# Retention and a low-rank mixer on one core: the second batch's unit work and the third batch's loads rearranged

## The chip, the core and the metric

The kernel runs on one core of one Trainium2 chip. A core has TensorE (PE in the profile: matrix products and transposes; PEld is its weight load), VectorE (DVE), ScalarE (ACT), GpSimd (POOL) and SyncE (SP), each with its own queue of instructions, and 16 DMA engines that all queues share. The metric is the device time of one execution in microseconds; the median of several runs is compared. One more execution was profiled, and all places and durations in this text come from its trace.

## The reference

```python
scores = q @ k^T / sqrt(64)                    # per batch (8), head (8); 576 positions, 64 wide
gamma  = 1 - 2 ** (-5 - head)
ret    = scores * (gamma ** (i - j) if i >= j else 0)
x      = ret @ v                               # heads side by side: (8, 576, 512)
h      = (x^T @ U @ V)^T                       # U: 576 x 32, V: 32 x 576
u      = x + h
out    = u + max(u @ w_ch1, 0) @ w_ch2         # w_ch1: 512 x 2048, w_ch2: 2048 x 512
```

The decay `gamma ** (i - j)` factors into a part for the query row and a part for the key row, so a key or a value can be scaled by its position before the product, and the result by the query's position after it.

## The kernel before, in words

Batches are taken in pairs. A pair has 2 x 576 = 9 x 128 rows, nine chunks; chunk 4 (called J) holds the end of the first batch and the start of the second. For pairs 1 to 3 each chunk is loaded (`load`, L227), cast (`cast_chunk`, L270), transposed by a DMA (`xbar`, L295) and used by `section` (L403: scores SC L312, values RV L332, running state). `prep` is cast and transpose together. The third batch is the first of pair 1; its chunks are `order[NI]`, `order[NI + 1]` and on.

Pair 0 is written out by hand in another form, so as to start early. The two batches are cut into four units of 256 rows, here called unit one to four (`u` = 0 to 3 in the code; units three and four are the second batch), and the chunk J. Unit work is:

- `load_u` (L621): k, q and v of a unit, each in two DMAs of 256 KB (four heads each), issued on SyncE. A memset by POOL into the first destination tile can hold them back: the DMA must wait for it, and what follows it on SyncE's queue waits too.
- `scale_u` (L653, instruction L655): the keys of four heads times a decay, f32 to bf16. `cast_u` (L646, L651): q or v of four heads to bf16.
- `T_u` (L662): transposes of k or q by TensorE (L671) into PSUM. With an engine named, all 16 land in one PSUM tile, which that engine copies out (L683 ScalarE, L685 VectorE). Without one they land in two tiles, copied by ScalarE (L680) and VectorE (L681) side by side. The PSUM tiles come from `ps_big`, three of them, which the Y1 blocks use as well.
- `SC_u` and `mask_u` (L700, L708): scores and their mask; `ST_u`, `Sblk` (L779, L789): the running state; `RV_u`, `QS_u`, `XS_u` (L727, L762, L770): values, the state's share, and the result scaled.

The feed-forward part is done per batch: 16 Y1 blocks (`u @ w_ch1`, L531, then Relu by ScalarE, L536), one for 128 columns of w1, and then Y2 (L565). w1 and w2 are loaded by POOL's own DMA queue (`load_w1` L196, `load_w2` L200), which converts f32 to bf16; `load_w1(f0, f1)` brings the columns of blocks f0 to f1 - 1. A Y1 block waits for its piece of w1.

`startup` (L881) has the first batch's units and all loads. Its loop at L947 is POOL's work for units three and four, with w1's pieces between, and then w2. `first_stretch` (L1003) is the second batch: `y(n)` puts the next n Y1 blocks of the first batch between the steps of `unit` (L1025), which has unit three and then unit four. Before it, L1049 issues the third batch's first loads (k, q and v of three chunks, k and q of a fourth) on SyncE, right behind unit four's. `merge` (L1083) then goes through Y1 of the second batch and Y2 of both and puts the third batch's casts, transposes and sections at given shares of that work. Order on each engine is the order written (`manual_schedule`); the stage buffers for f32 inputs are 15, used in turn.

Of the kernel before, what the change touches and what calls it, by code (L numbers as in the profile page):

```python
# [34 lines left out]
def kernel(  # L35
# [11 lines left out]
    nc = tc.nc  # L47
# [10 lines left out]
    NI = 9  # L58
# [105 lines left out]
    def load_v_rows():  # L164
        nc.sync.dma_start(out=V_f, in_=moe_V)
# [28 lines left out]
    def load_w1(f0, f1):  # L194
        w = slice(f0 * P, f1 * P)
        nc.gpsimd.dma_start(  # L196
            out=w1_sb[:, :, w], in_=moe_w_ch1[:, w].rearrange("(c p) f -> p c f", p=P))
# [16 lines left out]

    ch = {}

    def load(pr, i, which, seg=None):
        c = ch.setdefault((pr, i), {})
        for j in which:
            if ("f", j) not in c:  # L220
                c["f", j] = stage.tile([P, H, D], FP32, tag="stage", name="stage_t")
            dram = (q, k, v)[j]
            for n_seg, (rows, b, t0) in enumerate(parts(pr, i)):
                if seg is not None and n_seg != seg:
                    continue
                n = rows.stop - rows.start
                nc.sync.dma_start(  # L227
                    out=c["f", j][rows, :, :],
                    in_=dram[b, :, t0:t0 + n, :].rearrange("h s d -> s h d"),
                )  # L230
# [361 lines left out]
    order = [(pr, i) for pr in range(B // 2) for i in range(NI)]  # L592
# [53 lines left out]
    def cast_u(u, j, hh, eng):  # L646
        o, f = unit_views(u, j, hh)
        if eng is nc.scalar:
            nc.scalar.activation(out=o, in_=f, func=AF.Copy)
        else:  # L650
            eng.tensor_copy(out=o, in_=f)  # L651

    def scale_u(u, hh, eng):  # L653
        o, f = unit_views(u, 1, hh)
        eng.tensor_tensor(  # L655
            out=o, in0=f,
            in1=vscaleU[:, u, :, 4 * hh:4 * hh + 4].rearrange("p j h -> p h j")[
                :, :, :, None].to_broadcast([P, 4, 2, D]),
            op=ALU.mult,
        )  # L660
# [220 lines left out]
    def startup():  # L881
        load_u(0, (1, 0))
        load_v_rows()
        load_u(1, (1, 0))
        load_u(0, (2,))
        load(0, J, (1, 0), seg=0)
        load_u(1, (2,))
        load(0, J, (2,), seg=0)
        load_u_rows()
        load(0, J, (1, 0, 2), seg=1)  # L890
        load_u(2, (1, 0, 2))
        nc.gpsimd.memset(st["x", 0][HI, J, :], 0.0)

        warm(10)
        cast_unit(0)
        T_u(0, 1, nc.vector)
        un[0]["off"] = y1_tile(0)[:, 0:4, :].rearrange(
            "p (a x) (y i) -> p a (x y) i", x=2, i=P)
        nc.vector.memset(un[0]["off"][HI], 0.0)
        warm(5)  # L900
        nc.scalar.activation(out=V_b, in_=V_f, func=AF.Copy)
        T_u(0, 0, nc.scalar)
        make_v()
        warm(5)
        SC_u(0, 0, ps_sc, "psc")
        mask_u(0, 0)
        cast_unit(1)
        cast_u(0, 2, 0, nc.gpsimd)
        cast_u(0, 2, 1, nc.gpsimd)
        cast_u(1, 2, 0, nc.gpsimd)  # L910
        load_w1(0, 2)
        cast_u(1, 2, 1, nc.gpsimd)
        T_u(1, 1, nc.scalar)
        SC_u(0, 1, ps_o, "po")
        mask_u(0, 1)
        SC_off(0, ps_sc, "psc")
        warm(3)
        T_u(1, 0)
        SC_off(1, ps_o, "po")
        warm(3)  # L920
        SC_u(1, 0, ps_sc, "psc")
        mask_u(1, 0)
        cast_qk(0, J, LO, nc.scalar, nc.vector, decay=True)
        SC_u(1, 1, ps_o, "po")
        mask_u(1, 1)

        acc1 = pss_tile()
        ST_u(0, ALL, acc1, True)
        Sblk(acc1, 1)
        RV_u(0, 0)  # L930
        RV_u(0, 1)
        RV_off()
        XS_u(0)
        T_J(LO)
        acc2 = ps_big.tile([P, NHP, P], FP32, tag="big", name="pss2")
        ST_u(0, ALL, acc2, True)
        prep_v(0, J, LO)
        cast_urows()
        RV_u(1, 0)
        SC_J(LO)  # L940
        mask_J(LO)
        ST_u(1, LO, acc1, False)
        Sblk(acc1, 2)
        cast_qk(0, J, HI, nc.gpsimd, nc.gpsimd)
        prep_v(0, J, HI)
        load_w1(2, 4)
        for u in (2, 3):  # L947
            for hh in range(2):
                scale_u(u, hh, nc.gpsimd)
            load_w1(4 if u == 2 else 10, 6 if u == 2 else 12)  # L950
            for hh in range(2):
                cast_u(u, 0, hh, nc.gpsimd)
            load_w1(6 if u == 2 else 12, 8 if u == 2 else 16)
            if u == 2:
                load_u(3, (1, 0, 2), nc.gpsimd)
            cast_u(u, 2, 0, nc.gpsimd)
            cast_u(u, 2, 1, nc.gpsimd)
            if u == 2:
                load_w1(8, 10)
        for f in range(0, NF, 2):  # L960
            load_w2(f)
        RV_u(1, 1)
        QS_u(1, 0, 1)
        XS_u(1, 0, 1)
        ST_u(1, ALL, acc2, False)
        Sblk(acc2, 3)
        QS_u(1, 1, 2)
        XS_u(1, 1, 2)
        RV_J(LO)
        QS_J(3)  # L970
        XS_J(LO)

        xT = [ps_big.tile([P, dm], FP32, tag="big", name="xT") for _ in range(3)]
        xT.append(ps_sc.tile([P, dm], FP32, tag="psc", name="xT"))

        def to_xT(lo, hi):
            for i in range(lo, hi):
                for cc in range(NCC):
                    nc.tensor.matmul(
                        xT[cc][:, i * P:(i + 1) * P],  # L980
                        st["x", 0][:, i, cc * P:(cc + 1) * P], ident,
                        start=(i == 0), stop=True, skip_group_check=True,
                    )

        to_xT(0, 2)
        MA, _, _, _ = mixer_items(0, 0, split=True)
        MA((ps_o, "po"))
        to_xT(2, J)
        for cc in range(NCC):
            g = slice(cc * R, (cc + 1) * R)  # L990
            nc.tensor.matmul(
                xT[cc], st["a", 0][g, :], V4[g, HALF:HALF + 4 * P],
                start=False, stop=True, skip_group_check=True,
            )
        for cc in range(NCC):
            o = st["uT", 0][:, :, cc, :]
            i_ = xT[cc].rearrange("p (s t) -> p s t", t=P)
            if cc % 2 == 0:
                nc.scalar.activation(out=o, in_=i_, func=AF.Copy)
            else:  # L1000
                nc.vector.tensor_copy(out=o, in_=i_)

    def first_stretch():  # L1003

        ys = iter([fn for _, fn in y1_items(0)])

        def y(n):
            for _ in range(n):
                fn = next(ys, None)
                if fn is not None:  # L1010
                    fn()

        _, MH0, _, outs0 = mixer_items(0, 0, split=True)
        MA1, MH1, MT1, outs1 = mixer_items(0, 1, split=True)
        T_J(HI)
        y(1)
        make_u()
        SC_J(HI)
        mask_J(HI)
        y(1)  # L1020
        acc = pss_tile()
        ST_J(HI, acc)
        Sblk(acc, 0)

        def unit(u, slots, last):  # L1025
            T_u(u, 1, nc.vector)
            T_u(u, 0, nc.scalar)
            y(2)
            SC_u(u, 0, ps_sc, "psc")
            mask_u(u, 0)  # L1030
            y(1)
            ST_u(u, LO, acc, False)
            Sblk(acc, slots[1])
            SC_u(u, 1, ps_sc, "psc")
            mask_u(u, 1)
            y(1)
            if not last:
                ST_u(u, HI, acc, False)
                Sblk(acc, slots[2])
            RV_u(u, 0)  # L1040
            QS_u(u, 0, slots[0])
            QS_u(u, 1, slots[1])
            if last:
                RV_J(HI)
                XS_J(HI)
            RV_u(u, 1)
            XS_u(u)

        for g in range(NI, NI + 4):  # L1049
            load(*order[g], (1, 0, 2) if g < NI + 3 else (1, 0))  # L1050
        unit(2, (0, 1, 2), False)
        y(1)
        unit(3, (2, 3), True)
        y(1)
        MA1()
        y(1)
        MH1(outs1[0])
        y(2)
        MT1(outs1[0])
        MH1(outs1[1])  # L1060
        y(16)
        Y1, rest = y1_items(1, by_seg=True)
        Y1(0, 0)
        Y1(1, 0)
        MT1(outs1[1])
        MH0(outs0[0])
        Y1(2, 0)
        for f in range(3):
            Y1(f, 1)
        return rest[3:]  # L1070

    with tc.manual_schedule():
# [18 lines left out]
        g = NI + 7  # L1091
        for b in range(2, B):
            pr, par = divmod(b, 2)
# [37 lines left out]
```

## Time and profile before

| what | us |
|---|---|
| median of 5 runs (326.48 to 328.36) | 327.03 |
| the profiled execution's own time | 327.62 |
| its span, first to last instruction | 325.8 |
| TensorE busy | 312.0 (96%) |
| VectorE busy | 168.3 (52%) |
| ScalarE busy | 144.2 (44%) |
| POOL busy | 102.7 (32%) |
| Y1 products L531, 768 | 132.9 |
| Y2 products L565, 535 | 123.8 |
| L655 key scaling on POOL, 8, mean 1061 ns | 8.4 |
| L651 casts on POOL, 16, mean 645 ns | 10.1 |

Busy time is the sum of an engine's instructions; DMA issues do not count as busy. Times in the timelines are from the start of the span. The granted clock of TensorE was 1.000 over the whole span.

### The profile page before, as it was taken

How to read it: one execution, taken by the hardware profiler on the slowest of the kernel's cores; microseconds unless marked ns; L12 is line 12 of the kernel's file. 1: busy time of each engine (PE TensorE's matmuls, PEld its weight loads, DVE VectorE, ACT ScalarE, POOL GpSimd, SP SyncE). 2: the span in 40 equal slices, each digit the busy share in tenths (PEclk: the TensorE clock that was granted, in tenths of full speed). 3: DMA queues.
4: the chain of work that ended last, by engine and by line, in shares of the span. 5: the costliest groups of instructions: out<-in, count | busy, mean ns of one | idle time of the engine just before them, and what ended most of it. 6: DMA issues, size and time to landing. Idle time of an engine off the chain costs nothing.

```text
span 325.8 us, 9085 instructions
## 1 busy us (share of the span) xinstructions
PE 312.0 (96%) x3860; PEld 170.8 (52%) x3885; DVE 168.3 (52%) x332; ACT 144.2 (44%) x326; POOL 102.7 (32%) x171
## 2 busy tenths in 40 slices
PE   8998889999999999999999999999999999999996
PEld 3574545765444444456744444457644444467544
DVE  7664454427645477546754477555744476510012
ACT  3847547894011385038810484048800473047400
POOL 7587772243112733132321423142321500010000
PEclk9999999999999999999999999999999999999999
DMA  8999999999994988978997599969996440340012
GB/s 220 232 217 204 252 197 196 197 206 145 228 208 113 256 178 179 210 183 168 201 190 178 137 187 209 208 151 164 190 209 171 116 67 3 101 111 0 2 75 86
DMA packets 152904, 53.30 MB, mean 164 GB/s; under 512 B 132032, under 2 KB 150336, under 8 KB 152864
## 3 DMA queue, kind: packets, MB, share of 16 engines
q1 hardware_dynamic: 144512, 40.40, 66.6%
q0 software_dynamic: 8352, 12.32, 16.4%
q8 instruction: 30, 0.49, 0.7%
q14 instruction: 10, 0.08, 0.1%
HBM read 36.85 MB, written 9.44 MB: 142 GB/s over the span
## 4 chain that ended last, share of the span: by engine, by line
PE 76%; DMA 9%; SPq 5%; ACT 3%; DVE 2%; POOL 2%; issue 2%; DVEq 0%
PE ps_y L565 36%; PE ps_y L531 32%; DMA qkT<-qk 3%; SPq L633 3%; DMA w_sb<-in_moe_w_ch_dram 2%; DMA stage_t<-in_k_dram 2%; DMA stage_t<-in_v_dram 2%; PE pp L312 2%; DVE u L480 2%; SPq L227 1%; ACT y L536 1%; PE pp L332 1%; PE pp L344 1%; PE ps_y L576 1%; POOL qk L655 1%
## 5 line engine op out<-in xcount | busy, mean ns | idle before, releaser
L531 PE MATMUL ps_y<-uT,w_sb 128*128 128x256 bf16 (+2 forms) x768 | 132.9, 326 | 2.0 <-DMA w_sb<-in_moe_w_ch_dram 1.0
L536 ACT ACTIVATE y<-ps_y 128x384 bf16<-128x384 f32 (+2 forms) x192 | 89.6, 491 | 96.0 <-PE ps_y L531 94.9
L565 PE MATMUL ps_y<-w_sb,y 128*128 128x512 bf16 x535 | 123.8, 379 | 2.2 <-issue 1.1
L531 PEld LDWEIGHTS <-w_sb 128*128 128x128 bf16 x768 | 72.1, 98 | 50.0 <-issue 2.7
L565 PEld LDWEIGHTS <-y 128*128 128x128 bf16 x560 | 52.6, 98 | 61.1
L288 POOL TENSOR_TENSOR vt<-stage_t,vscale 64x256 bf16<-64x256 f32 (+1 forms) x81 | 50.2, 619 | 68.6 <-DMA stage_t<-in_v_dram 58.5
L554 DVE TENSOR_TENSOR o_sb<-ps_y,u 128x512 f32<-128x512 f32 (+2 forms) x38 | 25.2, 664 | 82.1 <-PE ps_y L565 79.8
L557 POOL DMA_DIRECT2D out_dram<-o_sb x31 | 17.2, 554 | 105.0 <-DVE o_sb L554 99.1
L320 DVE TENSOR_TENSOR ret<-pp,triH 128x512 bf16<-128x512 f32 x27 | 18.7, 692 | 24.0 <-PE pp L344 18.6
L480 DVE TENSOR_TENSOR u<-ph,xt 128x768 bf16<-128x768 f32 (+2 forms) x24 | 21.8, 951 | 5.9 <-PE ph L474 5.9
L279 DVE CAST qk<-stage_t 64x256 bf16<-64x256 f32 x54 | 19.1, 353 | 5.2 <-DMA stage_t<-in_k_dram 4.0
L453 ACT ACTIVATE a_sb<-pa 128x128 bf16<-128x128 f32 x8 | 2.2, 278 | 43.2 <-PE pa L447 43.2
L360 DVE TENSOR_TENSOR xt<-pp,qscale 128x512 bf16<-128x512 f32 x27 | 18.6, 690 | 4.7 <-PE pp L344 4.2
L399 DVE TENSOR_TENSOR s_sb<-AB,Af 64x256 bf16<-64x256 f32 x42 | 17.7, 422 | 2.1 <-ACT s_sb L394 1.5
L354 DVE COPY q<-qkT 64x256 bf16<-64x256 bf16 x48 | 13.2, 275 | 9.8 <-DMA qkT<-qk 8.8
L280 ACT ACTIVATE qk<-stage_t 128x512 bf16<-128x512 f32 x27 | 16.8, 621 | 0.6 <-DMA stage_t<-in_q_dram 0.6
L708 DVE TENSOR_TENSOR ret<-psc,triU 128x1024 bf16<-128x1024 f32 x8 | 9.7, 1222 | 9.7 <-PE psc L700 9.7
L392 ACT ACTIVATE Af<-AB 128x256 f32<-128x256 f32 x24 | 9.2, 385 | 8.1 <-PE AB L374 7.7
L651 POOL CAST qk<-stage_t 128x512 bf16<-128x512 f32 x16 | 10.1, 645 | 3.9 <-DMA stage_t<-in_v_dram 3.1
L312 PEld LDWEIGHTS <-qkT 64*64 64x64 bf16 x432 | 5.6, 107 | 10.8 <-issue 7.8
L277 ACT ACTIVATE qk<-stage_t 128x256 bf16<-128x256 f32 x27 | 11.0, 409 | 0.0
L655 POOL TENSOR_TENSOR qk<-stage_t,vscaleU 128x512 bf16<-128x512 f32 x8 | 8.4, 1061 | 5.4 <-PE psc L700 2.9
(121 smaller groups left out, 213.8 us busy)
## 6 DMA issues: line engine op xcount, KB each, us to landing
stage_t<-in_k_dram SPq DMA_DIRECT2D x32, 256.0 KB, 4.7
stage_t<-in_q_dram SPq DMA_DIRECT2D x32, 256.0 KB, 5.4
stage_t<-in_v_dram SPq DMA_DIRECT2D x32, 256.0 KB, 5.7
out_dram<-o_sb POOLq DMA_DIRECT2D x31, 256.0 KB, 3.5
w_sb<-in_moe_w_ch_dram POOLq DMA_DIRECT2D x14, 256.0 KB, 9.2
stage_t<-in_k_dram SPq DMA_DIRECT2D x8, 128.0 KB, 3.3
stage_t<-in_q_dram SPq DMA_DIRECT2D x8, 128.0 KB, 3.8
stage_t<-in_v_dram SPq DMA_DIRECT2D x8, 128.0 KB, 3.5
```

Source lines behind the costliest of these rows:

```text
L279: nc.vector.tensor_copy(out=o[to, hl], in_=f[fr, hl])
L280: nc.scalar.activation(out=c["qk"][:, 0, :], in_=c["f", 0].rearrange("p h d -> p (h d)"), func=AF.Copy)
L288: nc.gpsimd.tensor_tensor(out=o[to, hl], in0=f[fr, hl], in1=w[fr, hl, :, None].to_broadcast([n, NHP, D]), op=ALU.mult)
L320: nc.vector.tensor_tensor(out=ret.rearrange("p a b i -> p a (b i)").rearrange("p a (b i) -> p a b i", i=D), in0=pp[:, :, 0:NHP * D].rearra ...
L360: nc.vector.tensor_tensor(out=st["x", pr][:, i, :].rearrange("p (hp hl d) -> p hl hp d", hl=2, d=D), in0=pp[:, :, NHP * D:2 * NHP * D].rea ...
L399: nc.vector.tensor_tensor(out=S_[half(x), 1, :], in0=Bk[half(1 - x)], in1=Af[half(1 - x), now, :], op=ALU.add)
L480: nc.vector.tensor_tensor(out=st["u", par][:, i0 - base:i0 - base + n, w].rearrange("p s (c d) -> p c s d", c=2), in0=ph[k][:, :, 0:n, :], ...
L531: nc.tensor.matmul(ps[:, 0:n, :], w1_sb[:, cc, f * P:(f + 1) * P], st["uT", par][:, c0:c0 + n, cc, :], start=(cc == 0), stop=(cc == NCC - 1),)
L536: nc.scalar.activation(out=st["y1", par][:, f, c0 * P:(c0 + n) * P], in_=ps[:, 0:n, :].rearrange("p s t -> p (s t)"), func=AF.Relu)
L554: nc.vector.tensor_tensor(out=o_sb[:, 0:n], in0=ps[:, 0:n], in1=st["u", par][:, c, w], op=ALU.add)
L557: (nc.sync if last else nc.gpsimd).dma_start(out=out_flat[r0:r0 + P, w], in_=o_sb[:, 0:n])
L565: nc.tensor.matmul(ps, st["y1", par][:, f, c * P:(c + 1) * P], w2_sb[:, f, :], start=(f == 0), stop=(f == NF - 1),)
```

## The change

Five edits, all in the second batch's stretch:

- The keys' scaling of units three and four is split: heads 0 to 3 stay on POOL, heads 4 to 7 go to VectorE, unit three's after the first Y1 block of the stretch, unit four's after unit three's second mask.
- POOL's loop is written out in another order: w1 4-5 ahead of unit three's keys, unit four's loads behind w1 6-7.
- w1's blocks 8 to 11 come in one piece; before they came in two, the second behind unit four's keys.
- The first load of the third batch moves from L1050 into `startup`, behind w1 12-15, and gets a gate: a one-column memset by POOL, as unit four's loads have.
- q's transposes of units three and four use two PSUM tiles, copied by ScalarE and VectorE. One Y1 block fewer stands inside unit three, one more behind it; in unit four one of its two early blocks stands between k's and q's transposes.

```diff
-    def load(pr, i, which, seg=None):
+    def load(pr, i, which, seg=None, gate=None):
...
                 c["f", j] = stage.tile([P, H, D], FP32, tag="stage", name="stage_t")
+                if gate is not None:
+                    gate.memset(c["f", j][:, 0:1, 0:1], 0.0)
+                    gate = None
...
-        for u in (2, 3):
-            for hh in range(2):
-                scale_u(u, hh, nc.gpsimd)
-            load_w1(4 if u == 2 else 10, 6 if u == 2 else 12)
-            for hh in range(2):
-                cast_u(u, 0, hh, nc.gpsimd)
-            load_w1(6 if u == 2 else 12, 8 if u == 2 else 16)
-            if u == 2:
-                load_u(3, (1, 0, 2), nc.gpsimd)
-            cast_u(u, 2, 0, nc.gpsimd)
-            cast_u(u, 2, 1, nc.gpsimd)
-            if u == 2:
-                load_w1(8, 10)
+        load_w1(4, 6)
+        scale_u(2, 0, nc.gpsimd)
+        for hh in range(2):
+            cast_u(2, 0, hh, nc.gpsimd)
+        load_w1(6, 8)
+        load_u(3, (1, 0, 2), nc.gpsimd)
+        for hh in range(2):
+            cast_u(2, 2, hh, nc.gpsimd)
+        load_w1(8, 12)
+        scale_u(3, 0, nc.gpsimd)
+        for hh in range(2):
+            cast_u(3, 0, hh, nc.gpsimd)
+        load_w1(12, 16)
+        load(*order[NI], (1, 0, 2), gate=nc.gpsimd)
+        for hh in range(2):
+            cast_u(3, 2, hh, nc.gpsimd)
...
         y(1)
+        scale_u(2, 1, nc.vector)
         make_u()
...
             T_u(u, 1, nc.vector)
-            T_u(u, 0, nc.scalar)
-            y(2)
+            if last:
+                y(1)
+            T_u(u, 0)
+            y(1)
...
             mask_u(u, 1)
+            if not last:
+                scale_u(3, 1, nc.vector)
             y(1)
...
-        for g in range(NI, NI + 4):
+        for g in range(NI + 1, NI + 4):
             load(*order[g], (1, 0, 2) if g < NI + 3 else (1, 0))
         unit(2, (0, 1, 2), False)
-        y(1)
+        y(2)
         unit(3, (2, 3), True)
```

## The prediction

> **What bounds the kernel now.** I read the page first. TensorE is busy 312.0 of 325.8 us, so at most 13.8 us can be won, and only where TensorE stands idle. Next comes the list of what TensorE waits for: engine, line, what it waited for, us in total, times, longest.
>
> ```profile
> PE pst L671 <- POOL qk L651: 1.4, 2, 1.0
> PE pp L312 <- DMA qkT<-qk: 1.3, 3, 0.6
> PE ps_y L531 <- DMA w_sb<-in_moe_w_ch_dram: 1.0, 2, 0.6
> PE pa L447 <- DVE xt L770: 0.5, 1, 0.5
> ```
>
> The first and third are what the change works on: 1.4 us for the q casts of unit four, 0.61 us for w1 blocks 2-3, 0.42 us for w1 blocks 10-11. The second is the third batch, which starts while the second one ends. The timeline of TensorE (start, us, what, idle before it) puts them in order:
>
> ```profile
> 29.29 1.90 PE L531 MATMUL ps_y<-uT,w_sb 128*128 128x512 bf16 x8 [0.61 <-DMA w_sb<-in_moe_w_ch_dram]
> ...
> 38.43 0.28 PE L671 MATMUL pst<-ident,qk 128*128 128x128 bf16 x2 [0.97 <-POOL qk L651]
> 39.13 0.51 PE L671 MATMUL pst<-ident,qk 128*128 128x128 bf16 x6 [0.41 <-POOL qk L651]
> ...
> 44.01 1.04 PE L531 MATMUL ps_y<-uT,w_sb 128*128 128x512 bf16 x4 [0.42 <-DMA w_sb<-in_moe_w_ch_dram]
> ...
> 69.13 0.32 PE L312 MATMUL pp<-qkT 64*64 64x64 bf16 x16 [0.58 <-DMA qkT<-qk]
> ```
>
> The last of these decides. At 69.13 TensorE, after all the work that the change rearranges, waits for the first transposed chunk of the third batch. What it gains before 69.13 counts only if that transpose is also issued earlier. So I read SyncE's queue, which issues the third batch's loads and this transpose, in order:
>
> ```profile
> 34.38 1.64 SPq L227 DMA_DIRECT2D stage_t<-in_k_dram  x1
> 36.12 2.01 SPq L227 DMA_DIRECT2D stage_t<-in_q_dram  x1
> 38.18 3.29 SPq L227 DMA_DIRECT2D stage_t<-in_v_dram  x1
> ...
> 54.72 4.36 SPq L227 DMA_DIRECT2D stage_t<-in_k_dram  x1
> 59.17 2.62 SPq L227 DMA_DIRECT2D stage_t<-in_q_dram  x1
> ...
> 63.65 1.00 SPq L227 DMA_DIRECT2D stage_t<-in_q_dram  x1
> 64.83 2.12 SPq L295 DMA_TRANSPOSE qkT<-qk  x1
> ```
>
> Eleven loads stand ahead of the transpose. While w2 comes in, each issue takes SyncE up to 6.3 us where a free one takes 0.5 to 0.8: SyncE is held back by transfers not yet done. The casts that feed this transpose end at 62.0 (ScalarE L280), so its issue at 64.83 is set by the loads. Last, the DMA queues by stretch (q0 POOL's, q1 SyncE's; packets, MB, share of 16 engines' time), first 28 to 41.5 us, then 41.5 to 59 us:
>
> ```profile
> q1 hardware_dynamic: 4885, 2.01, 58.8%
> q0 software_dynamic: 2066, 1.04, 58.8%
> ...
> q0 software_dynamic: 2682, 2.58, 88.9%
> q1 hardware_dynamic: 3290, 0.83, 30.3%
> ```
>
> In both stretches the shares sum to nearly 1.2, which is as high as this trace goes: the DMA engines are full, except 61 to 63 us, where the table by stretch gives 94 GB/s and a share of 0.44.
>
> **What the Trainium skill says.** "DMA: Bandwidth & Descriptors", Queues, rings and completion order: each DMA engine goes round-robin between the queues that have work. The trace agrees: 2682 packets of q0 beside 3290 of q1 from 41.5 to 59, so while w2 runs a third-batch packet passes for about each w2 packet. The same page, Why small descriptors are slow: a packet carries a fixed overhead. Agreed: from 28 to 38 us q0's 1552 packets of w1 (512 bytes) take 58.5% of 160 engine-us, 60 ns each; from 41.5 to 59 the packets of mostly 1024 bytes take 0.889 x 280 / 2682 = 93 ns. "GPSIMD Engine Reference", Engine selection: a two-input elementwise operation is about 2x slower there than on VectorE. Agreed: L655 on POOL is 1061 ns, a 128x512 product on VectorE (L770) 0.69 us.
>
> **The change part by part.**
>
> *Half the key scaling on VectorE.* POOL loses two L655 of 1.06 us, VectorE gains two of about 0.69 us. The trace has no such form on VectorE with both inputs in SBUF; between 0.6 and 0.75 us, I take 0.69. The first sits in VectorE's idle 0.78 us before 26.26 and is free; if it ran 0.1 us over, the mask behind it (L827) would move by as much, which has over 2 us until its use. The second is queued after the mask of unit three, done at 34.68. It waits for unit four's second k tile, which landed at 35.68, so VectorE is held until about 36.4. Behind it stand L770 of unit three, moved from 36.09 to 36.4, and the k copy L685, from 37.50 to about 37.7; the scores that need them start at 41.30. TensorE wants these keys at 36.85: spare 0.45 us, and a k tile later than that costs one for one.
>
> *POOL's order.* One L655 less before unit three's q casts: they end near 27.1 instead of 28.1, w1 6-7 goes out at 27.1 instead of 28.05, the gate of unit four's loads opens at 27.9 instead of 28.79, so its k is issued at 28.0 instead of 28.92. w1 4-5 is issued at 24.0 instead of 26.13, but w1 2-3, the transfer waited for at 29.29, keeps its place: the 0.61 us stay.
>
> *w1 8 to 11 in one piece.* Half as many packets: 2 x 512 x 60 = 61.4 engine-us become 512 x 93 = 47.6, a saving of 13.8 / 16 / 1.2 = 0.7 us of full DMA time. It goes out at about 29.2, where 10-11 went at 36.75: the 0.42 us at 44.01 go. Its price is on q1: those packets are 33 ns longer and alternate with unit four's k and q, 512 x 33 / 16 = 1.05 us. That eats the 0.9 us of earlier issue; q of unit four lands as before, near 37.7 and 38.2, within 0.7 us either way.
>
> *q^T through two banks, Y1 blocks moved.* One 1.31 us copy (L683) becomes a 0.74 us half on ScalarE beside a 0.73 us half on VectorE, as L680 and L681 took for unit two; a Y1 block covers either, so nothing is won. Only the block order pays: one Y1 block (1.0 us) moves between unit four's k and q transposes, into the 1.38 us of idle. Casts end at about 38.8 (39.07 now), the transposes at 39.3; 0.9 to 1.0 us are won. The number of blocks stays the same.
>
> Sum ahead of 69.13: 0.95 + 0.42 = about 1.4 us.
>
> *The third batch gated.* Its first load now waits for a memset on POOL behind unit four's q casts and w1 12-15. Casts to 38.8, the issue 0.75 us, the memset 0.1: the first load goes out near 39.8 instead of 34.38, and all eleven loads and the transpose stand behind it on SyncE. (The memset itself waits for nothing: its buffer is free since POOL's last L252, at 23.3. Behind it on POOL stand two v casts and w2, which lose its 0.1 us.) The transfers have room for this only if the DMA engines have other work. Now they have not: unit four's loads run out near 38.2 (v landed by 39.76, when its cast started); w1 12-15, issued near 38.9, starts moving some 1.6 us later (w1 4-5, issued at 26.13, landed at 30.7, its 256 KB taking 1.9 us at 140 GB/s and the landing some more). I take 2.3 us without transfers (bounds 1.2 and 3.0). Cross-check by bytes: of 2.01 MB on q1 up to 41.5, 1.57 MB are unit four's six loads; the other 0.44 MB are third batch, 1.9 us at the 227 GB/s of 63 to 65 us. Given back: 0.7 us for the longer piece and about 0.5 us of gaps between the earlier w1 pieces (rate down to 39 GB/s near 29.3). Net 2.3 - 0.7 - 0.5 = +1.1 us for the eleventh load, and for the transpose at 64.83, now near 65.9.
>
> *The end.* From the transpose on everything is a chain: landing 4.3 us later, TensorE starts L312 near 70.2, having waited 0.58 + 1.1 + 1.4 = 3.1 us. The next transpose (70.46) follows after five SyncE issues and moves as far; its wait of 0.40 us stays. Behind 80 us the list of waits has none above 0.4 us, so nothing absorbs it. Sum: +1.1 us on the profiled execution, 327.62 us (span 325.8), so 328.7; the median of the runs is 0.6 us lower, so **328.1 us**.
>
> **Rivals.** *The early transpose (faster).* The DMA lull of 61 to 63 us is worth 1.1 us, and it shows SyncE late with issues, not DMA full. If w2, now less disturbed, ends sooner and SyncE catches up at 0.8 us a load there, the eleventh load is not late. Place: the transpose's issue; the whole changes by its shift, down to the gain of TensorE, 1.4 + 0.58 = 2.0 us, the most. It decides at 64.83: issued at 63.3 gives -1.5 us, 325.5. Against: 0.44 MB must still pass behind w2. *The balance.* Lull and idle cancel and the transpose is within 1 us of its place: 327.0; what TensorE gains turns into its wait at L312. *The gate alone, without givebacks*, or q landing 0.7 us late, which delays the gate too: +2.3, 329.3; I count it with the slower case. That the Y1 blocks hide nothing is possible too, but it matters only in the faster case.
>
> **How the numbers follow.** Late transpose 0.46, balance 0.24, early transpose 0.30. What this kernel's measurement can tell from no change is about 0.3%, 1 us. The late case itself spans 328.0 to 329.8; the range for 8 in 10 takes in the early one to 325.2 and the late one to 330.0. Slower 0.46, same 0.24, faster 0.30.
>
> **What would show it.** In the changed trace: no wait at the q transposes above 0.4 us, none for w1 10-11; the first third-batch k issued near 39.8; a dip of DMA between 38 and 41; the first L295 near 65.9 and a wait of some 3 us at L312. If L295 comes before 64.5 the forecast is wrong, and the gain ahead of it counts.

## The result, and the profile after

| | executions | median us |
|---|---|---|
| kernel before | 50 | 327.32 (325.91 to 330.79) |
| changed kernel | 29 | 328.84 (325.23 to 331.83) |

By medians the changed kernel is 1.52 us (0.46%) slower, where the prediction had 1.1. The ratio of the two kernels is 1.0003, 95% interval 0.9981 to 1.0025; it leaves out executions more than 1.5% above the fastest of their kernel (8 of the 30 recorded for the changed kernel), while the medians take in all. Both together say: not clearly different, perhaps slower. The forecast's range, 325.2 to 330.0, holds the median; its sign, slower, shows in the medians alone. The profiled execution took 329.15 us (span 327.4). Lines after 217 of the file have moved, those named here by 3: L312 is now L315, L531 is L534, L227 is L230, L651 is L654.

TensorE's waits from 20 to 85 us in the changed kernel (engine, line, waited for, us in total, times, longest):

```profile
PE ps_y L534 <- DMA w_sb<-in_moe_w_ch_dram: 1.9, 1, 1.9
PE pp L315 <- DMA qkT<-qk: 1.8, 2, 1.5
PE pa L450 <- DVE xt L773: 0.5, 1, 0.5
```

The two waits for unit four's q casts (1.4 us before) and the one for w1 10-11 are gone. The wait for the third batch's transposes has grown from 1.0 us in this stretch to 1.8. The one wait for w1 2-3, 0.61 before, was 1.9 in this execution. The timeline of TensorE, changed kernel:

```profile
30.51 1.04 PE L534 MATMUL ps_y<-uT,w_sb 128*128 128x512 bf16 x4 [1.86 <-DMA w_sb<-in_moe_w_ch_dram]
...
32.05 1.89 PE L534 MATMUL ps_y<-uT,w_sb 128*128 128x512 bf16 x4
...
40.90 0.61 PE L674 MATMUL pst<-ident,qk 128*128 128x128 bf16 x8
...
70.91 0.32 PE L315 MATMUL pp<-qkT 64*64 64x64 bf16 x16 [1.52 <-DMA qkT<-qk]
```

Unit four's q transposes (40.90) run without a wait; but TensorE comes to them 2.5 us later than before (38.43), and the Y1 block moved ahead of them is only 1.0 us of that. The long wait for w1 and a slow stretch at 32 us are in it, so this profile doesn't show what the edit did there. The third batch's first scores start at 70.91 instead of 69.13. A Y1 block at 32.05 takes 1.89 us where the one at 30.51 took 1.04; that is TensorE's clock, and comes up below. SyncE's queue, changed kernel:

```profile
41.05 0.37 SPq L230 DMA_DIRECT2D stage_t<-in_k_dram  x1
41.51 0.53 SPq L230 DMA_DIRECT2D stage_t<-in_q_dram  x1
...
65.38 1.25 SPq L230 DMA_DIRECT2D stage_t<-in_q_dram  x1
66.81 2.07 SPq L298 DMA_TRANSPOSE qkT<-qk  x1
```

The gate opens at 41.05 (first load at 34.38 before), the eleventh load is out at 66.6, and the first transpose at 66.81 instead of 64.83. The DMA engines from 38 to 41 us, changed kernel, as the rate in 40 slices of 0.075 us and the bytes of SyncE's queue:

```profile
GB/s 341 335 342 341 348 328 341 348 321 321 266 266 266 219 451 177 164 123 123 137 137 96 75 61 41 41 48 41 48 41 41 41 34 27 7 0 0 0 0 0
...
q1 hardware_dynamic: 927, 0.46, 50.9%
```

They run dry just before the gate opens. In the kernel before no slice of the same stretch fell under 184 GB/s.

### The profile page after: what moved, and what is told of

It is laid out like the page before. It is cut to its first block, busy times and chain, and to the rows that moved or that the text cites. A ratio compares the mean times of both kernels' runs of the same rounds, so it can differ in the third digit from the quotient of the medians.

```text
span 327.4 us, 9076 instructions
## 1 busy us (share of the span) xinstructions
PE 312.4 (95%) x3860; PEld 171.2 (52%) x3885; DVE 171.9 (53%) x336; ACT 142.9 (44%) x326; POOL 99.4 (30%) x169
## 4 chain that ended last, share of the span: by engine, by line
PE 76%; DMA 9%; SPq 6%; ACT 3%; DVE 3%; issue 2%; POOL 0%; DVEq 0%
PE ps_y L568 33%; PE ps_y L534 33%; DMA qkT<-qk 4%; SPq L636 3%; PE pp L315 2%; DMA w_sb<-in_moe_w_ch_dram 2%; DMA stage_t<-in_v_dram 2%; DVE u L483 2%; SPq L230 2%; ACT y L539 1%; DMA stage_t<-in_q_dram 1%; PE pp L335 1%; PE pp L347 1%; PE ps_y L579 1%; PE AB L377 1%
## 5 line engine op out<-in xcount | busy, mean ns | idle before, releaser
L534 PE MATMUL ps_y<-uT,w_sb 128*128 128x256 bf16 (+2 forms) x768 | 133.8, 328 | 3.1 <-DMA w_sb<-in_moe_w_ch_dram 1.9
L534 PEld LDWEIGHTS <-w_sb 128*128 128x128 bf16 x768 | 72.3, 98 | 51.1 <-issue 3.5
L654 POOL CAST qk<-stage_t 128x512 bf16<-128x512 f32 x16 | 9.7, 616 | 8.5 <-PE ps_y L534 4.3
L315 PEld LDWEIGHTS <-qkT 64*64 64x64 bf16 x432 | 5.6, 107 | 11.7 <-issue 7.8
L315 PE MATMUL pp<-qkT 64*64 64x64 bf16 x432 | 8.6, 198 | 2.2 <-DMA qkT<-qk 2.2
```

What stands on the lines that cost most here:

```text
L315: nc.tensor.matmul(pp[half(m), m ^ hl, hp * D:(hp + 1) * D], qkT[half(hl), NHP + hp, half(m)], qkT[half(hl), hp, half(m ^ hl)], start=True ...
L534: nc.tensor.matmul(ps[:, 0:n, :], w1_sb[:, cc, f * P:(f + 1) * P], st["uT", par][:, c0:c0 + n, cc, :], start=(cc == 0), stop=(cc == NCC - 1),)
```

## The experiments

Each kernel was timed beside the kernel before on the same chip; the first four shared one chip, the next four another, then three, then one. "Lowered clock" counts executions whose mean granted TensorE clock was 0.996 or less. An interval that holds 1 shows no clear difference; four don't hold it (the gate alone, both fillers, both mends). Medians from different chips are compared below only with care: the kernel before itself lies between 327.45 and 328.50 on these four.

| kernel | median us | before, same chip | ratio (95%) | lowered clock |
|---|---|---|---|---|
| changed, again | 328.96 | 327.45 | 1.0018 (0.9991 to 1.0045) | 12 of 22 |
| changed, ungated | 327.06 | 327.45 | 0.9986 (0.9962 to 1.0010) | 4 of 22 |
| before + gate | 328.35 | 327.45 | 1.0029 (1.0007 to 1.0051) | 9 of 22 |
| ungated, fewer loads ahead | 327.31 | 327.45 | 0.9988 (0.9959 to 1.0016) | 4 of 14 |
| before + TensorE order | 327.96 | 327.81 | 1.0002 (0.9976 to 1.0027) | 2 of 14 |
| changed + filler at the scores | 329.32 | 327.81 | 1.0027 (1.0005 to 1.0048) | 3 of 22 |
| changed + filler at w1 | 331.26 | 327.81 | 1.0105 (1.0069 to 1.0142) | 4 of 6 |
| ungated, two transposes first | 327.07 | 327.81 | 0.9990 (0.9968 to 1.0012) | 3 of 22 |
| changed, gate before the keys | 326.91 | 327.51 | 0.9986 (0.9961 to 1.0011) | 6 of 22 |
| changed, w1 8-11 in two pieces | 328.91 | 327.51 | 1.0018 (0.9991 to 1.0044) | 9 of 22 |
| before + two transposes first | 327.35 | 327.51 | 0.9986 (0.9963 to 1.0009) | 4 of 22 |
| changed, both mends | 327.25 | 328.50 | 0.9954 (0.9921 to 0.9987) | 3 of 13 |

The kernel before had a lowered clock in 17 of 67, 14 of 51, 17 of 59 and 9 of 18 executions on the four chips.

### The changed kernel again

> The changed kernel itself, beside the other three. Theory (the gate delays the third batch): the first transpose of the third batch is issued near 66.8 us, 2.0 us later than before, and TensorE starts the first scores of the third batch (L315) near 70.9; time +1 to +2 us on the kernel before. Rival (the change is neutral, and the profiled run was an unlucky one with TensorE's clock lowered near 32 us): time within 1 us of before, and L315 near 69.

The median is 1.5 us above that of before, with the same wide spread (325.2 to 331.9); the ratio, 1.0018, is not clear of 1. Its own profile has no long w1 wait, so the wait at the scores stands alone (TensorE's timeline):

```profile
69.63 0.43 PE L315 MATMUL pp<-qkT 64*64 64x64 bf16 x16 [2.37 <-DMA qkT<-qk]
...
70.21 5.86 PE L534 MATMUL ps_y<-uT,w_sb 128*128 128x384 bf16 x32
76.00 0.32 PE L315 MATMUL pp<-qkT 64*64 64x64 bf16 x16
```

TensorE is at the scores at 67.26 (69.63 - 2.37), 1.3 us earlier than before (69.13 - 0.58 = 68.55), and leaves them 0.5 us later. And the 32 products behind take 5.86 us, where before they took 4.68. The table by stretch of this kernel (TensorE's granted clock is the number ahead of the last two) shows why:

```profile
63.00:69.60 6.60, 4.26 (x31) 2.82 (x29) 1.09 (x2) 4.94 (x13) 3.67 (x6) 1.00 1.10 219
69.60:73.00 3.40, 3.37 (x35) 2.05 (x36) 1.71 (x5) 2.01 (x5) 1.71 (x3) 0.51 1.17 202
73.00:76.00 3.00, 3.00 (x25) 2.03 (x23) 0.44 (x2) 2.24 (x6) 0.26 (x1) 1.00 1.27 192
```

After the long wait the clock is at half for 3.4 us, which costs 3.4 x 0.49 = 1.7 us of TensorE's work. POOL's timeline shows the chain that opens the gate: the casts wait for q, then come w1 12-15 and the memset.

```profile
37.89 1.29 POOL L654 CAST qk<-stage_t 128x512 bf16<-128x512 f32 x2 [3.83 <-DMA stage_t<-in_q_dram]
39.12 0.80 POOL L196 DMA_DIRECT2D w_sb<-in_moe_w_ch_dram  x1
39.92 0.12 POOL L223 MEMSET stage_t<- 128x1 f32 x1
```

In the first profile the same casts waited longer, and the wait is put down to TensorE, which was late there:

```profile
38.89 1.26 POOL L654 CAST qk<-stage_t 128x512 bf16<-128x512 f32 x2 [4.33 <-PE ps_y L534]
```

So the gate seems able to open late for two reasons, a late q and a late TensorE.

### The gate taken out, and the gate alone

Ungated:

```diff
-        load(*order[NI], (1, 0, 2), gate=nc.gpsimd)
...
-        for g in range(NI + 1, NI + 4):
+        for g in range(NI, NI + 4):
```

> The changed kernel without the gate: the third batch's first load is again issued on SyncE behind unit four's. Theory (gate): the first third-batch transpose is issued no later than 64.8 us; TensorE reaches it 1.0 to 1.4 us earlier than before and waits there, so the time is that of before or up to 1 us less, and 1 to 2 us less than with the gate. Rival (the loss lies in the other four edits): as slow as with the gate.

The kernel before with the gate alone, behind w1 12-15 in the loop at L947 (`load` gets its `gate` as in the change; not shown again):

```diff
             if u == 2:
                 load_u(3, (1, 0, 2), nc.gpsimd)
+            else:
+                load(*order[NI], (1, 0, 2), gate=nc.gpsimd)
...
-        for g in range(NI, NI + 4):
+        for g in range(NI + 1, NI + 4):
```

> The kernel before with the gate alone (the third batch's first load behind POOL's memset that follows w1 12-15). Theory: the first third-batch transpose is issued 1.5 to 2.5 us later than before and the kernel is slower by 1.2 to 2.5 us, since TensorE waits only 0.58 us there in the kernel before. Rival (a lull of the DMA engines at 61 to 63 us takes up the delay): within 0.7 us of before.

On one chip, taking the gate out of the changed kernel lowers the median from 328.96 to 327.06, and putting it into the kernel before raises it from 327.45 to 328.35. The second is clear of 1 (1.0029), though 0.9 us is less than the 1.2 to 2.5 expected; the ratios of the first pair, 1.0018 and 0.9986, have intervals that overlap. SyncE's queue with the gate alone:

```profile
41.71 0.37 SPq L230 DMA_DIRECT2D stage_t<-in_k_dram  x1
...
67.03 2.06 SPq L298 DMA_TRANSPOSE qkT<-qk  x1
```

The scores start at 71.23 there, after 1.35 us of wait; ungated, at 68.31. The profiles of all kernels with eleven loads ahead of the transpose, ordered by the start of their first load (us; kernels not yet named follow below):

| kernel | first load | first transpose | wait at the scores |
|---|---|---|---|
| changed, gate before the keys | 33.68 | 62.59 | none |
| before + TensorE order | 33.83 | 64.26 | 1.11 |
| before | 34.38 | 64.83 | 0.58 |
| changed, ungated | 34.48 | 64.24 | 0.65 |
| changed, w1 8-11 in two pieces | 38.66 | 64.46 | none |
| changed + filler at w1 | 40.04 | 65.15 | 1.97 |
| changed, again | 40.07 | 65.48 | 2.37 |
| changed | 41.05 | 66.81 | 1.52 |
| changed + filler at the scores | 41.21 | 66.41 | 0.57, behind the filler |
| before + gate | 41.71 | 67.03 | 1.35 |

In the last six lines the gate stands behind the casts. There the transpose goes out 25.1 to 25.8 us after the first load, so a later gate means a later transpose. In the one profile where it opens at 38.7 the transpose is not late; where it opens at 40 to 42 it is 0.3 to 2.2 us later than in the kernel before. So the gate is what delays the transpose, in both surroundings, and with the gate out the loss in the medians is gone. The rival that the lull at 61 to 63 takes up the delay holds in part only: in the changed kernel the first load is 6.7 us later and the transpose 2.0; the lull is gone (233 GB/s there, 94 before), and the transpose is late all the same. Ungated, a second thing shows that the prediction only bounded: unit four's second k tile came late, VectorE scaled it at 36.08, and TensorE waited 0.67 us for it.

### Fewer loads ahead of the transpose

The gate is out here too; shown is what differs from the ungated kernel:

```diff
-        for g in range(NI, NI + 4):
-            load(*order[g], (1, 0, 2) if g < NI + 3 else (1, 0))
+        for g in range(NI, NI + 3):
+            load(*order[g], (1, 0, 2))
...
-            [(0.04, ready(0)), (0.05, fetch(3, (2,))), (0.06, fetch(4, (1, 0))),
+            [(0.04, ready(0)), (0.05, fetch(3)), (0.06, fetch(4, (1, 0))),
```

> The changed kernel without the gate, and with k and q of the third batch's fourth chunk loaded behind the first transpose instead of ahead of it. Theory (TensorE waits for a transpose whose issue is held up by the loads ahead of it on SyncE): the transpose is issued near 62.8 us, two loads or 1.8 us earlier than before, the wait at the first scores is gone, and what TensorE gained before counts: 1.5 to 2.0 us faster than before. Rival (the later loads then hold up the next chunks' transposes as much): within 0.7 us of before.

The transpose went out at 61.61 and the scores had no wait. Yet the kernel is no faster than the ungated one: the next two chunks' scores waited 0.75 and 0.69 us, since the second transpose (70.41) stood behind seven loads. The expected 1.5 to 2.0 us did not come; the rival was right.

### TensorE's order alone

```diff
             T_u(u, 1, nc.vector)
-            T_u(u, 0, nc.scalar)
-            y(2)
+            if last:
+                y(1)
+            T_u(u, 0)
+            y(1)
...
         unit(2, (0, 1, 2), False)
-        y(1)
+        y(2)
```

> The kernel before with the order of TensorE alone changed: q's transposes of units three and four through two PSUM tiles, and the Y1 blocks moved. POOL's order, w1's pieces and the third batch's loads stay. Theory (what TensorE wins ahead of the first third-batch transpose counts only up to the 0.58 us of wait that stand there in the kernel before, since the transpose is not issued sooner): TensorE reaches that wait about 0.9 us earlier, waits there about 1.4 us, and the time changes by less than 0.5 us. Rival (the gain counts in full): 0.9 us faster.

Ratio 1.0002, so the 0.9 us of the rival did not come in full (lower end of the interval 0.9976, or 0.8 us). In its profile the q transposes had no wait, TensorE reached the scores at 67.13, 1.4 us earlier than before, and waited 1.11 us there, 0.5 us longer than before. The rest of the 1.4 us counted in this one execution (326.36 us), for its transpose, at 64.26, was also 0.6 us earlier. Over 14 executions nothing is left: what is won ahead of this wait and doesn't move the transpose is lost in it.

### Work put into the two waits

```diff
             mixing(2, 0.16, 0.70, (0.71, 0.77)),
+            [(0.2049, lambda: warm(7))],
```

> The changed kernel, with seven more 128x512 products (about 1.6 us of work that nothing reads) on TensorE just ahead of the third batch's first scores, where it waits 1.5 to 2.4 us. Theory (the delayed transpose costs twice: the wait, and after a wait of 2 us and more TensorE's clock drops to half for some 3.4 us, worth 1.7 us): the filler fits in the wait and keeps the clock up, the share of executions with a lowered clock falls from about one in two to one in four, as before the change, and the median falls by 0.5 to 1 us against the changed kernel. Rival (the lowered clock has its place earlier, at the wait for w1 near 29 us): share and median as in the changed kernel or up to 0.5 us above.

```diff
             T_u(u, 0)
+            if not last:
+                warm(4, ps_o, "po")
             y(1)
```

(`warm` is also given its PSUM tiles as arguments, not shown.)

> The changed kernel, with four more 128x512 products (about 0.9 us of work that nothing reads) on TensorE ahead of the Y1 block that waits for w1 2-3 near 29 us (0.6 to 1.9 us of wait). If the lowered clock comes from this wait: the share of executions with a lowered clock falls to one in four or less and the median by 0.5 to 1 us. If it comes from the wait at the third batch's first scores: both stay as in the changed kernel.

The filler at the scores does what it should to the clock: 3 of 22 executions with a lowered clock; without it, on another chip, 12 of 22 (and 14 of the 30 with a recorded clock in the first measurement). Its lines (TensorE's timeline, then the clock by stretch):

```profile
68.44 1.67 PE L191 MATMUL pw<-ident 128*128 128x512 bf16 x7
70.68 0.32 PE L315 MATMUL pp<-qkT 64*64 64x64 bf16 x16 [0.57 <-DMA qkT<-qk]
```

```profile
68.00:74.00 6.00, 5.43 (x58) 3.38 (x56) 2.03 (x5) 4.26 (x11) 3.34 (x6) 1.00 1.20 208
```

But the median is not lower (329.32; 328.96 on the other chip), and the 0.5 to 1 us expected did not come: with the clock kept up, this kernel is still 1.5 us over the kernel before on its own chip. One reason may be that the filler takes 1.67 us in every execution, also where the wait would have been shorter; no run shows that. So the wait at the scores is one place of the clock drops, but not the only one: of the five profiles with a lowered clock, two have the drop there (the changed kernel again, and the filler at w1), three near 30 us (the changed kernel's first, the gate alone, w1 in two pieces). And that the drop is the larger part of the 1.5 us is not shown. The filler at w1 leaves 4 of 6 executions with a lowered clock, the profile's own at 70 to 74 us, and adds its 0.9 us and more. Six executions show only that it doesn't help.

### Two transposes first

Here k and q of the fourth chunk follow the first transpose, and all other loads the second (the loop of the fewer-loads version, and):

```diff
-            [(0.04, ready(0)), (0.05, fetch(3, (2,))), (0.06, fetch(4, (1, 0))),
-             (0.12, ready(1)), (0.13, fetch(4, (2,))), (0.20, ready(2)), (0.28, ready(3)),
+            [(0.04, ready(0)), (0.05, fetch(3, (1, 0))),
+             (0.12, ready(1)), (0.125, fetch(3, (2,))), (0.13, fetch(4)), (0.20, ready(2)), (0.28, ready(3)),
```

In the ungated changed kernel:

> The changed kernel without the gate; on SyncE nine third-batch loads, the first transpose, the fourth chunk's k and q, the second transpose, and only then the loads that follow. Theory (TensorE waits for transposes held up by the loads ahead of them): the first is issued near 61.6 us, the second near 66.5, no wait above 0.2 us at either scores, and the time is 0.7 to 1.2 us below the kernel before and below the changed kernel without the gate. Rival (a later transpose is then held up, as the second was when only the first was moved): within 0.4 us of the changed kernel without the gate.

In the kernel before:

> The kernel before, with the third batch's fourth chunk loaded behind its first transpose and the following loads behind the second; nothing of the change. Theory (the wait for the transposes bounds this stretch, and without it TensorE is ahead only by what it won before): the 0.58 and 0.40 us of wait go, 0.5 to 1.0 us faster than before. Rival (as in the version that had the change's other edits, part of the wait comes back at the third chunk): within 0.4 us of before.

Both removed the waits at the first two scores and left about 0.5 us at the third. Medians are 0.7 and 0.2 us below before, neither ratio clear of 1; the 0.5 to 1.0 us expected of the second did not come, and its rival, within 0.4 us, fits the medians. The first has the ungated kernel's median (327.07 and 327.06, on two chips), as its rival said. The difference between the two, what the other four edits may be worth once the waits are gone, is too small for these intervals.

### The gate moved ahead of the casts

```diff
         load_w1(8, 12)
+        load(*order[NI], (1, 0, 2), gate=nc.gpsimd)
         scale_u(3, 0, nc.gpsimd)
...
-        load(*order[NI], (1, 0, 2), gate=nc.gpsimd)
```

> The changed kernel with the gate's memset moved on POOL: behind w1 8-11 and ahead of unit four's keys, so that it no longer stands behind the casts that wait for unit four's q. Theory (the gate costs because it waits for q, and the DMA engines run empty meanwhile): the third batch's first load is issued near 34.5 us as in the kernel before, there is no lull at 38 to 41 us, the first transpose is issued near 64.3, and the median is that of the changed kernel without a gate, 1 to 2 us under the changed kernel. Rival (the order of the loads against w1 12-15 matters, not the wait): still near 66.

The gate is still there, but no longer behind a wait for q. SyncE's queue in this kernel:

```profile
33.68 0.77 SPq L230 DMA_DIRECT2D stage_t<-in_k_dram  x1
...
62.59 1.92 SPq L298 DMA_TRANSPOSE qkT<-qk  x1
```

The scores start at 67.72 without a wait, from 38 to 41 us the DMA engines move 260 GB/s, and the median is 326.91, 2 us under the next version's (the changed kernel with two w1 pieces, 328.91), on the same chip. The ratios of the two, 0.9986 and 1.0018, point the same way, with intervals that overlap. So what costs is where the gate stands, not that there is one. The edit moves it ahead of two things, the wait for q and the issue of w1 12-15; no run parts them.

### The long piece of w1

```diff
-        load_w1(8, 12)
+        load_w1(8, 10)
+        load_w1(10, 12)
```

> The changed kernel with w1 8-11 in two pieces again, issued one after the other at the place of the long one. The prediction gave the long piece 0.7 us of DMA time that reaches the transpose. If so: transposes 0.7 us later, 0.5 to 0.7 us slower than the changed kernel. Rival (the DMA engines run empty before the gate opens, so time saved ahead of that is lost in the lull): transposes and median as in the changed kernel, within 0.3 us, and w1 10-11 still in time.

328.91: no loss to be seen against the changed kernel (328.84 and 328.96 on other chips; the ratios are equal, 1.0018, each uncertain by 0.9 us). The median fits the rival, but its reason is not borne out: in this kernel's own profile q came early, the gate opened at 38.66, there was no lull (237 GB/s from 38 to 41 us), and the transpose went out at 64.46. Whether the time saved by the long piece ends up in the lull stays open.

### Both mends

> The changed kernel with both mends: the gate's memset ahead of unit four's keys, and on SyncE only nine third-batch loads ahead of the first transpose, the fourth chunk's k and q behind it, the other loads behind the second. Theory (the late transposes are all that the change loses): no wait at the first scores, share of executions with a lowered clock at or under one in four, median 0.6 to 1.2 us under the kernel before. Rival (each mend alone removes the wait, so the two do not add): as the version with the gate moved alone, within 0.3 us, 0.6 us under the kernel before.

The gate ahead of the keys and two transposes first: 0.9954, interval 0.9921 to 0.9987, the only version clearly faster than the kernel before, by 1.25 us in the median. The kernel before was itself slower on this chip than on the others (328.50, a lowered clock in 9 of 18 executions), and one clear case among twelve comparisons should be taken with care. It stayed at full clock in 10 of 13 executions, and its first two scores had no wait. It was not timed beside the changed kernel on one chip, but its ratio lies under the changed kernel's 1.0003 and 1.0018. Whether it is better than either mend alone, the intervals don't tell.

## Why the prediction was right, point by point

- *TensorE waits for the first third-batch transpose, and only its issue counts.* Right: with TensorE's order alone no gain was left over 14 executions, ratio 1.0002.
- *The gate delays that issue.* Right: 65.9 was forecast for the transpose, 65.48 and 66.81 were measured in two profiles of the changed kernel, and the gate alone gave 67.03. The gate-only ratio, 1.0029, is 0.95 us. The lull at 38 to 41 us, the ground of the +1.1, stands in both profiles of the changed kernel (158 and 46 GB/s). The changed kernel's own ratios, 1.0003 and 1.0018, don't part this case from the *balance* rival, and 65.48 would fit that one too; it is the gate alone and the table of first loads that speak for the late case.
- *The balance of that sum.* The gate opened later than 39.8, at 40.07 and 41.05, once, by the profile, because TensorE was late, which the sum left out. The 0.7 us "given back" by the longer piece was not seen (two pieces, same median within 0.9 us). The transpose moved by 0.65 and by 1.98 us; that the forecast of +1.1 lies between them is in part luck.
- *Gains ahead of the wait, 1.4 us.* Of the q casts' 1.38 us, the changed kernel's second profile still had 0.59 and 0.40: q landed later relative to TensorE than the term assumed. The 0.42 us of w1 10-11 was gone in both profiles of the changed kernel, but also in three kernels that keep the two pieces where they were (the gate alone, TensorE's order alone, before with two transposes first); so it was a chance of one execution more than a term of the sum. Arrival at the scores was 1.3 us earlier in the second profile, close to the forecast, though most of the wait for q was still there; the sum came out by luck in part. In the first, with a lowered clock at 31 to 35 us, 0.8 us later (69.39).
- *The 0.61 us at w1 2-3 stay.* They did not: the wait was 1.86 us in the changed kernel's first profile and none for w1 in its second, and up to 1.74 in others with POOL's new order, against at most 0.88 in the four kernels with the old one. The reason is open, and so is what it costs.
- *Wait of 3.1 us at the scores.* Too large: 1.52 and 2.37, for in the first profile TensorE came 2.2 us later than forecast, and in the second the transpose went out 0.4 us earlier.
- *VectorE's key scaling.* 0.69 and 0.68 us in the first profile, as taken from L770, but up to 1.15 us in others, for a reason that stays open; hidden in the changed kernel's first profile, 0.67 us of wait in the ungated one, the price named for a late k tile.
- *Two readings.* The prediction called 1061 ns on POOL against 0.69 us on VectorE agreement with a factor of about 2; it is 1.5. And 1.2 is not the highest DMA share of the trace: from 38 to 41 us it is 1.36 in the kernel before.
- *Behind 80 us nothing absorbs it.* The loss remained, but a part was missing: the prediction had no term for TensorE's clock. Half of the changed kernel's executions (26 of 52) had a lowered clock, against 57 of 195 of the kernel before; with the gate alone it was 9 of 22. Of the 30 executions of the first measurement with a recorded clock, those with a lowered clock had a median of 329.95 us, the others 326.96. The forecast of 328.1 against 328.84 has its error of 0.7 us in the direction of this term; how much of it the clock caused is open, for executions with a long wait have both the wait and the drop.

## What to carry to other kernels

Before adding up what an edit wins, find the next wait behind it that the edit doesn't move; the gain stops there, and what counts is whether the edit delays the thing waited for. A gate that holds loads back should open on something that is sure to be early: put behind work that waits for a load itself, it can let the DMA engines run dry. Everything behind a gated load on its queue is delayed with it, the transposes too. And one profile is one execution: the gate opened anywhere from 38.7 to 41.7 us, so a wait that one profile shows or lacks is not yet an effect of the edit.

## What the runs showed of the hardware

In five of the profiled executions TensorE's granted clock went to about half for some 3.4 us and came back; for example 0.51 over 69.6 to 73.0 us, behind 2.37 us of idle, and in the changed kernel's first profile, behind 1.86 us:

```profile
31.30:34.70 3.40, 3.40 (x30) 1.60 (x28) 1.23 (x1) 1.19 (x2) 1.05 (x1) 0.53 1.07 253
```

Each drop cost TensorE some 1.7 us of work (3.4 x 0.49), about as much as the waits themselves. A drop near 30 us is not all lost, for TensorE then comes later to the scores and waits less there: 1.52 us in the changed kernel's first profile, none with w1 in two pieces, against 2.37 us. One wait of 2 us is not needed. With the gate alone no single wait was longer than 0.87 us, but four of them, 2.2 us in all, came within some 3 us (TensorE's timeline, then the clock from 30 to 32 us):

```profile
27.57 0.28 PE L674 MATMUL pst<-ident,qk 128*128 128x128 bf16 x2 [0.43 <-POOL qk L658]
28.59 0.51 PE L674 MATMUL pst<-ident,qk 128*128 128x128 bf16 x6 [0.73 <-POOL qk L658]
29.97 0.39 PE L674 MATMUL pst<-ident,qk 128*128 128x128 bf16 x2 [0.87 <-POOL qk L654]
30.52 0.82 PE L674 MATMUL pst<-ident,qk 128*128 128x128 bf16 x6 [0.15 <-POOL qk L654]
```

```profile
30.00:32.00 2.00, 1.84 (x11) 1.04 (x12) 0.00 (x0) 0.62 (x1) 2.00 (x5) 0.50 1.05 130
```

With w1 in two pieces a wait of 1.34 us, 0.40 us of idle not long before it, was enough, with the filler at w1 one of 1.97. Single waits of 1.50 us (filler at the scores), 1.52 (the changed kernel's first, at the scores) and 1.74 (both mends) were followed by full clock. So it seems that the idle time within a few us counts and not one wait alone; and as much idle time brings a drop in one execution and none in another. The Trainium skill, "TensorE: Matmul & The Clock Gate", Part 1, tells of a clock halved after an idle window of about 3.4 us, with windows that run freely; the length of the drop agrees, but here idle of 1.7 to 2.4 us in all, in one piece or with work between, was enough.
